# A memory-recurrent attention kernel: last projection rows two at a time, softmax sums in column tiles, a new order of work in a segment, weights loaded from the second quarter on

## The chip, the cores and the metric

The kernel runs on one core of one Trainium2 chip. The metric is the device time of a whole execution in microseconds; I give medians of several executions. The times of the kernel before lie within 0.3 to 0.8% of one another, by round (1616.15 to 1620.62 us in one of seven executions, 1615.40 to 1627.98 in another), those of a variant below, in its fast runs, within 0.1 to 0.9%. A profile shows one execution, and its span is some 2 us shorter than the time of the same execution (1627.2 us against 1628.95 for the changed kernel). The record counts all the timed runs that I compare as fast, except one that is named (1636.07 us at a granted clock of 0.957); the two kernels that had one look only have no state in it.

## The reference, cut to what matters

```python
# A: 64 segments of 32 tokens; an 8-token memory is carried from one segment to the next
for s in range(n_seg):
    h = concat([mem, x[:, 32 * s:32 * s + 32]])        # 40 tokens, 576 features
    q, k, v = h @ Wq, h @ Wk, h @ Wv                   # 32 heads of 128
    p = softmax(where(mask, q @ k.T * scale, -1e9))
    o = (p @ v) @ Wo
    mem, out = o[:8], o[8:]
# B: ordinary attention over 2048 tokens, 32 heads of 18
# result: g * A + (1 - g) * B with g = sigmoid(x . gate_w)
```

A is serial: a segment needs the memory of the one before. B is parallel, and the kernel cuts it into 512 steps (scores `sb`, exponential, values `ob`), of which it lays 7 or 8 beside each segment of A.

Of the kernel before, what the change touches and what calls it, by code (L numbers as in the profile page):

```python
# [16 lines left out]
def kernel(  # L17
# [77 lines left out]
    def weights(name):  # L95
        return (
            aw1.tile([P, NF, HD], BF16, name=name + "_m"),
            aw1.tile([P, HD // 2], BF16, name=name + "_t"),
        )

    wv, wq, wk = weights("wv"), weights("wq"), weights("wk")

    def load_weights(w, src):
        w2 = src.rearrange("d h e -> d (h e)")
        for c in range(NF):
            yield nc.gpsimd.dma_start(out=w[0][:, c, :], in_=w2[c * P:(c + 1) * P, :])
        for two in range(2):
            yield nc.gpsimd.dma_start(
                out=w[1][TL * two:TL * two + TL, :],
                in_=w2[NF * P:Dm, two * (HD // 2):(two + 1) * (HD // 2)],  # L110
            )

    def w_slice(w, c, f0, n):

        if c < NF:
            return w[0][:, c, f0:f0 + n], c
        f1 = f0 % (HD // 2)
        return w[1][:, f1:f1 + n], NF + f0 // (HD // 2)
# [143 lines left out]
    loads, first_loads = nc.sync, []  # L262
# [37 lines left out]
    def last_tokens(q, share, k=None):  # L300
# [8 lines left out]
        for b in range(HD // 512):  # L309
            pv = bank(k[0], [P, 512], FP32, "pv")  # L310
            for c in range(NF + 1):
                rw, cc = w_slice(wv, c, b * 512, 512)
                nc.tensor.matmul(pv[:, :], lhsT=xlb[:, cc, :], rhs=rw, start=(c == 0), stop=(c == NF))  # L313
            vl = stage()
            yield
            copy_out(vl[:, :], pv[:, :], share)
            store.dma_start(out=vld[q * P:(q + 1) * P, b * 512:(b + 1) * 512], in_=vl[:, :])
            yield
# [143 lines left out]
    for t in range(NQC):  # L462
        for n in range(4 * t, 4 * t + 4):
# [23 lines left out]

    load_first()
    ready.extend([first_loads[-1]] * 2)
# [23 lines left out]
    def between(cost):  # L513
        spare[0] += cost
        if spare[0] >= 1.8:
            spare[0] -= 1.8
            b_advance(1)

    for blk in FIRST:
        store_qk(blk, range(1, GB))  # L520
    for kb in range(NKB):
        project_vb(1, kb, 3)
# [10 lines left out]
    for q in range(4):  # L533
        in_turn(
            nc.gpsimd.dma_start(
                out=wo[:, 8 * q:8 * q + 8, :], in_=A_Wo[8 * q:8 * q + 8].rearrange("h e d -> e h d")
            )
        )
    fix = actx.enter_context(tc.tile_pool(name="fix", bufs=1))
    seg2 = actx.enter_context(tc.tile_pool(name="seg2", bufs=2))  # L540


    def pad(g):
        for t in (qtd, ktd):
            nc.gpsimd.dma_start(out=pads(t, g), in_=pads(t, 0))

    pad(1)


    for i, _ in enumerate(last_tokens(0, 1 << 30)):  # L550
        if i % 2:
            between(1.1)
    loads = nc.gpsimd

    fill_bank = [0]

    def later_tokens():
        for q in range(1, n_seg // SG):
            yield from last_tokens(q, 0, fill_bank)

    later = later_tokens()


# [70 lines left out]
    put_x(0)  # L634

# [102 lines left out]
    def segment(s, banks):  # L738
# [11 lines left out]
        def project(x, w, b, k):  # L750
            pv = bank(k, [P, 512], FP32, "pvv")
            for c in range(NF + 1):
                for j in range(4):
                    rw, cc = w_slice(w, c, (2 * (j // 2) + b) * 1024 + (j % 2) * 512, 512)
                    nc.tensor.matmul(  # L755
                        pv[32 * j:32 * j + 32, :],
                        lhsT=ht[:, cc, :],
                        rhs=rw,
                        start=(c == 0),
                        stop=(c == NF),  # L760
                        tile_position=(0, 32 * j),
                    )
            ps[x] = pv
# [56 lines left out]
        def sums(b, k):  # L820
            ps["p", b] = bank(k, [P, 512], FP32, "pss")
            nc.tensor.matmul(ps["p", b][:, 0:W8], lhsT=bsel[:, :], rhs=et[:, b, :], start=True, stop=True)  # L822
# [79 lines left out]
        for x, w in (("Q", wq), ("K", wk), ("V", wv)):  # L902
            for b in range(2):
                step(f"{x}{b}", project, f"{x}{b}", w, b, banks[f"{x}{b}"])
                step(f"c{x}{b}", copy, f"{x}{b}")
        for b in range(2):
# [30 lines left out]
        for i in range(3):  # L937
# [9 lines left out]
        Q0 cQ0 K0 B E : cK0 / K1 tq0 tk0 pq0 V0 cK1 B E : pk0 Q1 S0 cV0 v0 cQ1 x0 tk1 n0 B E : tq1 pk1  # L947
        V1 pq1 p0 cV1 v1 l0 r0 / S1 m0 B F1 w00 x1 n1 o00 F2 cF1 p1 w01 E : B l1 cF2 o01 r1 m1 E : F0
        a00 w10 cF0 w11 B E : o10 o11 ol a01 a10 a11 B / E : h0 g0 h1 g1 f0 ht0 f1 ht1 og oh
        """.split(),  # L950
        8: """
        Q0 B E : V0 cQ0 K0 cV0 v0 B / cK0 E : tq0 pq0 Q1 tk0 pk0 cQ1 B / E : S0 K1 tq1 x0 cK1 B n0 tk1 E
        : V1 pk1 pq1 p0 cV1 v1 S1 l0 r0 x1 / B E : F0 m0 n1 w00 o00 F1 cF0 p1 w01 o01 cF1 l1 r1 m1 B F2
        a00 cF2 w10 o10 w11 E : B E : o11 ol a01 a10 h0 a11 g0 B h1 g1 f0 E : f1 ht0 ht1 oh og
# [4 lines left out]
            A0=0, A1=1, F0=2, F1=0, F2=1, K0=2, K1=0, Q0=1, Q1=2, S0=0, S1=1, V0=1, V1=0, p0=2, p1=2,  # L959
            pv=0, pw=2, t0=2, t1=1, w00=2, w01=0, w10=1, w11=2,  # L960
        ),
        8: dict(
            A0=2, A1=0, F0=0, F1=1, F2=0, K0=0, K1=2, Q0=2, Q1=1, S0=0, S1=1, V0=1, V1=2, p0=0, p1=2,
            pv=0, pw=1, t0=2, t1=1, w00=2, w01=0, w10=1, w11=0,
# [3 lines left out]
    LOAD_LAST = "r1"  # L968
# [163 lines left out]
```

## The kernel before: the parts that the change touches

A segment projects its first 32 tokens here, in four column tiles; the last 8 tokens of every segment are projected ahead, for 16 segments together (`last_tokens`, the fill-in of the loop). Of the 576 rows of a weight, four chunks have 128; the last 64 take a fifth pass, in which half of the array works on zeros.

```python
def project(x, w, b, k):
    pv = bank(k, [P, 512], FP32, "pvv")
    for c in range(NF + 1):                 # NF = 4 full chunks and the last 64 rows
        for j in range(4):                  # four column tiles at a time
            rw, cc = w_slice(w, c, (2 * (j // 2) + b) * 1024 + (j % 2) * 512, 512)
            nc.tensor.matmul(pv[32 * j:32 * j + 32, :], lhsT=ht[:, cc, :], rhs=rw,
                start=(c == 0), stop=(c == NF), tile_position=(0, 32 * j))
    ps[x] = pv

def copy(x):
    sbt[x] = seg2.tile([P, 512], BF16, name="tm", bufs=4)
    nc.vector.tensor_copy(out=sbt[x][:, :], in_=ps[x][:, :])
```

The order of a segment is a list of names. `Q0` to `V1` are projections, `cQ0` their casts, `tq0`, `pq0` transposes of queries and their copies, `S` scores, `x`, `l`, `r` three ScalarE operations of the softmax, `n`, `m` two of VectorE, `p` sums, `w` weighing, `a` output projection, `f`, `ht` the next memory, `F1`, `F2` the fill-in, `B` and `E` the two halves of a step of B.

```python
8: """
Q0 B E : V0 cQ0 K0 cV0 v0 B / cK0 E : tq0 pq0 Q1 tk0 pk0 cQ1 B / E : S0 K1 tq1 x0 cK1 B n0 tk1 E
: V1 pk1 pq1 p0 cV1 v1 S1 l0 r0 x1 / B E : F0 m0 n1 w00 o00 F1 cF0 p1 w01 o01 cF1 l1 r1 m1 B F2
a00 cF2 w10 o10 w11 E : B E : o11 ol a01 a10 h0 a11 g0 B h1 g1 f0 E : f1 ht0 ht1 oh og
""".split(),
```

The start-up stores queries and keys, then the second half of the values, then projects the rest with steps of B between:

```python
for blk in FIRST:
    store_qk(blk, range(1, GB))
for kb in range(NKB):
    project_vb(1, kb, 3)
for blk in (1, 6, 2, 7, 3, 8):
    for t in range(NQC):
        project_qk(blk, t, 0)
        between(1.1)                        # a step of B when 1.8 us have gathered
# ... loads of Wo, padding copies, last tokens of 16 segments, then the set-up of the segments
```

The softmax here doesn't subtract the row's maximum and nothing guards it: scores larger than these inputs give would overflow.

## Time and profile before

| | kernel before |
|---|---|
| time, median | 1619.4 us |
| profiled span, mean granted clock | 1613.9 us, 0.986 |
| start of the first segment (first `Q0`) | 174.55 us |
| start of the last segment | 1558.28 us |
| segments with 7 steps | 28 of 64 |

The prediction below shows the main views. Two more are needed for the explanation, and I had not read them before I predicted. The first is busy time by stretch: window, length, then busy us of TensorE, weight loads, VectorE, ScalarE and GpSimd with their counts, then the granted clock (1.00 is full), DMA share and GB/s. The lines are 22 segments with 7 steps, 19 with 8 steps and fill-in, and the last 16 without fill-in.

```profile
174.55:657.68 483.13, 454.87 (x8119) 239.43 (x8119) 305.79 (x755) 339.67 (x286) 101.96 (x221) 0.99 0.22 52
789.15:1212.97 423.82, 409.63 (x7276) 213.78 (x7277) 265.48 (x663) 327.10 (x266) 87.20 (x190) 1.00 0.21 47
1212.97:1558.28 345.31, 315.00 (x5744) 160.33 (x5742) 210.18 (x537) 274.46 (x225) 55.50 (x130) 1.00 0.17 35
```

TensorE is busy for 409.63 of 423.82 us, 97%, in the second. The waits of TensorE in 680 to 1200 us agree (who waited, for whom: us in all, times, longest):

```profile
PE pw L879 <- DVE hl L657: 4.6, 15, 0.4
PE pvv L755 <- DVE ht L891: 4.4, 9, 0.5
PE sb L238 <- ACT etb L257: 4.2, 12, 0.6
```

All the waits of that view come to less than 20 us in 520.

### The profile page before, as it was taken

The numbers are of one execution on the slowest core, as the hardware profiler recorded it, in microseconds if no ns is written. First come the engines' busy times: TensorE is split into PE (matmuls) and PEld (weight loads), VectorE is DVE, ScalarE is ACT, GpSimd is POOL, SyncE is SP. The second block draws the span as 40 slices with busy tenths as digits, with TensorE's granted clock in tenths as the row PEclk, the third lists the DMA queues.
The fourth block names the chain that finished last, engine by engine and source line by source line (L and its number), as shares of the span: only waits on it lengthen the run. The fifth ranks groups of instructions, "written<-read, shape, count | busy, mean of one in ns | idle before, by whom it ended". The sixth has DMA issues, their size and how long they took to land.

```text
span 1613.9 us, 57766 instructions
## 1 busy us (share of the span) xinstructions
PE 1476.7 (91%) x25082; PEld 782.0 (48%) x25082; DVE 960.0 (59%) x2355; ACT 1139.8 (71%) x981; POOL 338.4 (21%) x731
## 2 busy tenths in 40 slices
PE   6598899999999999999999999999999989998997
PEld 3434444555454444555454445555554444444445
DVE  2233666666566666666566666666666656565656
ACT  2165577777677767777677777777777777788774
POOL 6311211213131031302121211212121212120131
PEclk9899999999999999999999999999999999999999
DMA  7788322212122121212122121212221121211125
GB/s 200 235 291 290 100 65 64 49 42 52 45 50 53 32 53 38 61 36 49 43 43 60 38 50 40 57 39 45 51 53 35 30 48 34 45 34 35 29 59 162
DMA packets 209865, 114.39 MB, mean 71 GB/s; under 512 B 159491, under 2 KB 197251, under 8 KB 208019
## 3 DMA queue, kind: packets, MB, share of 16 engines
q1 hardware_dynamic: 188971, 58.40, 16.1%
q0 software_dynamic: 19696, 50.02, 9.9%
q8 instruction: 196, 3.21, 0.9%
q10 hardware_dynamic: 944, 2.29, 0.4%
q14 instruction: 58, 0.48, 0.1%
HBM read 60.94 MB, written 36.10 MB: 60 GB/s over the span
## 4 chain that ended last, share of the span: by engine, by line
PE 69%; ACT 11%; DVE 11%; DMA 4%; issue 2%; SPq 1%; POOL 1%; DVEq 0%; ACTq 0%; POOLq 0%
PE pvv L755 27%; ACT etb L257 9%; PE sb L238 8%; PE ob L222 7%; PE pt L782 5%; PE pv L326 4%; PE psh L800 3%; PE acc L643 3%; PE pso L838 3%; PE pv L313 2%; DVE hl L657 2%; PE pq L420 2%; DVE hl L654 2%; DVE ot L850 2%; ACT rq L830 2%
## 5 line engine op out<-in xcount | busy, mean ns | idle before, releaser
L257 ACT ACTIVATE etb<-sb 128x2048 bf16<-128x2048 f32 x512 | 959.6, 1874 | 341.9 <-PE sb L238 341.1
L767 DVE CAST tm<-pvv 128x512 bf16<-128x512 f32 x384 | 264.4, 689 | 175.1 <-PE pvv L755 174.2
L755 PEld LDWEIGHTS <-ht 128*32 128x32 bf16 x7680 | 185.8, 97 | 183.7 <-DVE ht L891 14.1
L238 PE MATMUL sb<-qch,kch 32*128 32x512 bf16 x2048 | 203.2, 386 | 38.5 <-ACT etb L257 36.7
L222 PE MATMUL ob<-etb,vch 128*32 128x512 bf16 x2048 | 205.9, 392 | 3.9 <-DVE tq L159 3.9
L850 DVE CAST ot<-pso 128x320 bf16<-128x320 f32 x256 | 120.7, 488 | 104.2 <-PE pso L838 99.9
L643 PE MATMUL acc<-wo,ot 128*32 128x384 bf16 (+1 forms) x4096 | 159.7, 291 | 5.4 <-DVE ot L850 3.3
L755 PE MATMUL pvv<-wq_m,ht 128*32 128x512 bf16 x2048 | 134.2, 382 | 13.0 <-DVE ht L891 8.3
L755 PE MATMUL pvv<-wk_m,ht 128*32 128x512 bf16 x2048 | 134.9, 384 | 0.0
L755 PE MATMUL pvv<-wv_m,ht 128*32 128x512 bf16 x2048 | 134.3, 382 | 0.0
L643 PEld LDWEIGHTS <-ot 128*32 128x32 bf16 x4096 | 105.2, 98 | 46.5 <-DVE ot L850 12.8
L700 POOL DMA_DIRECT2D a_dram<-rl x186 | 92.6, 506 | 162.4 <-DVE rl L695 143.3
L238 PEld LDWEIGHTS <-kch 32*128 32x128 bf16 x2048 | 61.2, 91 | 128.5 <-issue 107.9
L857 POOL COPY otl<-ot 128x256 bf16<-128x256 bf16 x64 | 25.9, 405 | 445.6 <-DVE ot L850 445.6
L222 PEld LDWEIGHTS <-vch 128*32 128x32 bf16 x2048 | 52.9, 93 | 120.6 <-issue 116.0
L782 PE MATMUL pt<-ident,tm 128*128 128x128 bf16 x1024 | 96.8, 221 | 0.8 <-DVE tm L767 0.8
L790 DVE COPY kt<-pt 128x512 bf16<-128x512 bf16 x128 | 54.0, 422 | 69.4 <-PE pt L782 69.0
L838 PE MATMUL pso<-et,v_sb 64*128 64x40 bf16 x2048 | 81.4, 178 | 14.9 <-DVE hll L657 4.7
L838 PEld LDWEIGHTS <-v_sb 64*128 64x128 bf16 x2048 | 62.8, 93 | 62.4 <-issue 49.5
L654 DVE CAST hl<-acc 128x384 bf16<-128x384 f32 (+1 forms) x128 | 57.9, 452 | 58.1 <-PE acc L643 57.8
L782 PEld LDWEIGHTS <-tm 128*128 128x128 bf16 x1024 | 57.8, 98 | 67.0 <-issue 49.4
L826 ACT ACTIVATE lt<-pss 128x320 f32<-128x320 f32 x128 | 56.0, 438 | 43.2 <-PE pss L822 32.8
(141 smaller groups left out, 1847.4 us busy)
## 6 DMA issues: line engine op xcount, KB each, us to landing
v_sb<-tm SPq DMA_DIRECT2D x512, 32.0 KB
wo<-in_A_Wo_dram POOLq DMA_DIRECT2D x4, 1152.0 KB, 9.7
wv_m<-in_A_Wv_dram POOLq DMA_DIRECT2D x4, 1024.0 KB, 8.0
wq_m<-in_A_Wq_dram POOLq DMA_DIRECT2D x4, 1024.0 KB, 9.1
wk_m<-in_A_Wk_dram POOLq DMA_DIRECT2D x4, 1024.0 KB, 8.0
xl<-qld SPq DMA_DIRECT2D x64, 64.0 KB
xl<-kld SPq DMA_DIRECT2D x64, 64.0 KB
v_sb<-vld SPq DMA_DIRECT2D x128, 32.0 KB
```

Of the source, the lines that this page charges most:

```text
L222: nc.tensor.matmul(ob[32 * j:32 * j + 32, :], lhsT=vc[:, o + 32 * j:o + 32 * j + 32], rhs=et4[:, j, :], start=(kb == 0), stop=(kb == NKB - 1),
L238: nc.tensor.matmul(sb[:, j, :], lhsT=kc[32 * j:32 * j + 32, o:o + P], rhs=qch[gq][32 * j:32 * j + 32, :], start=True, stop=True, tile_posi ...
L257: nc.scalar.activation(out=before[:, :, :], in_=sb[:, :, :], func=ACT.Exp, scale=scale_b)
L326: nc.tensor.matmul(pv[:, o:o + P], lhsT=lw, rhs=xlb[:, cc, :], start=(c == 0), stop=(c == NF))
L643: nc.tensor.matmul(acc[32 * j:32 * j + 32, 0:d1 - d0], lhsT=o[:, h, 0:CT], rhs=wo[:, h, d0:d1], start=(b == 0 and i == 0), stop=(b == 1 an ...
L654: nc.vector.tensor_copy(out=hl[:, 0, d0:d1], in_=acc[:, 0:d1 - d0])
L700: eng.dma_start(out=rows4[m, seg - LO:seg, i * n:(i + 1) * n], in_=rl[32 * i + m * LO:32 * i + (m + 1) * LO, :],)
L755: nc.tensor.matmul(pv[32 * j:32 * j + 32, :], lhsT=ht[:, cc, :], rhs=rw, start=(c == 0), stop=(c == NF), tile_position=(0, 32 * j),)
L767: nc.vector.tensor_copy(out=sbt[x][:, :], in_=ps[x][:, :])
L782: nc.tensor.transpose(out=pt[:, which, :, :, :].rearrange("p j (u i) t -> p j u i t", i=4)[:, :, :, i, :], in_=sbt[x][:, i * Dh:(i + 1) * Dh],
L838: nc.tensor.matmul(pso[:, i * L:(i + 1) * L], lhsT=v_sb[64 * jj:64 * jj + 64, b * 1024 + i * Dh:b * 1024 + (i + 1) * Dh], rhs=et[64 * jj:6 ...
L850: nc.vector.tensor_copy(out=ot[:, j * HG:(j + 1) * HG, :].rearrange("p h t -> p (h t)"), in_=ps["o", b, jj][:, 0:W8],)
```

## The change

Its intent: two projections share one pass for their last 64 rows, one in the upper and one in the lower half of the array, so that six tail passes become three; softmax sums and the fill-in's values are cut into column tiles like their neighbours, so that the tile shape changes less often; a new order puts the first projections and steps densely one after another; in the start-up, part of the weights is loaded between 20 and 60 us, the values are stored ahead of queries and keys, fewer steps of B stand there, and the set-up of the segments goes ahead of the last tokens. The core of the diff:

```diff
-        def project(x, w, b, k):
-            pv = bank(k, [P, 512], FP32, "pvv")
-            for c in range(NF + 1):
+        def project(x, w, b):
+            first = begin(x)
+            for c in range(NF):
                 ...
+        def project_tails(two):
+            two = [(x, w, b, begin(x)) for x, w, b in two]
+            for j in range(4):
+                for x, w, b, first in two:
+                    t, r = w_tail(w, columns(b, j), 512)
+                    nc.tensor.matmul(
+                        ps[x][32 * j:32 * j + 32, :],
+                        lhsT=ht[TL * r:TL * r + TL, NF + r, :],
+                        rhs=t[TL * r:TL * r + TL, :],
+                        start=first, stop=(not first),
+                        tile_position=(TL * r, 32 * j),
+                        skip_group_check=True,
+                    )
... (sums and the fill-in's values: one matmul becomes four column tiles)
+        step("T0", project_tails, (("Q0", wq, 0), ("K0", wk, 0)))
+        step("T1", project_tails, (("Q1", wq, 1), ("K1", wk, 1)))
+        step("T2", project_tails, (("V0", wv, 0), ("V1", wv, 1)))
... (order of 8 steps; that of 7 likewise)
-        Q0 B E : V0 cQ0 K0 cV0 v0 B / cK0 E : tq0 pq0 Q1 tk0 pk0 cQ1 B / E : S0 K1 tq1 x0 cK1 B n0 tk1 E
-        : V1 pk1 pq1 p0 cV1 v1 S1 l0 r0 x1 / B E : F0 m0 n1 w00 o00 F1 cF0 p1 w01 o01 cF1 l1 r1 m1 B F2
-        a00 cF2 w10 o10 w11 E : B E : o11 ol a01 a10 h0 a11 g0 B h1 g1 f0 E : f1 ht0 ht1 oh og
+        Q0 B T0 / cQ0 V1 T2 E : cV1 v1 B E : V0 K0 cV0 v0 B E : Q1 cK0 tk0 / tq0 T1 pq0 B K1 E : cQ1 pk0
+        cK1 S0 tq1 x0 B E : pq1 tk1 n0 pk1 S1 x1 p0 / l0 r0 n1 F1 p1 m0 cF1 F0 cF0 l1 r1 m1 B E : w00
+        w01 o00 o01 w11 w10 a00 B E : o10 o11 a01 h0 g0 a10 a11 F2 ol h1 B g1 cF2 E : f0 ht0 f1 ht1 oh
+        og
... (start-up)
+        for _ in range((0, 1, 2, 2)[t]):
+            next(pieces)                    # pieces of the weights, from the second quarter on
-        if spare[0] >= 1.8:
-            spare[0] -= 1.8
+        if spare[0] >= 2.15:
+            spare[0] -= 2.2
+    for kb in range(NKB):
+        project_vb(1, kb, 3)
     for blk in FIRST:
         store_qk(blk, range(1, GB))
-    for kb in range(NKB):
-        project_vb(1, kb, 3)
... (loads of Wo, padding copies and the last tokens move behind the set-up of the segments)
```

## The prediction

> **What bounds the kernel now.** I read the page, then busy time by stretch, then the timeline and the chain of waits of each stretch. The run has three stages: a start-up up to 174.5 us (transposes, projections of attention B, last tokens of the first 16 segments), 64 recurrent segments up to about 1572 us, and the final projection. The chain that ended last is mainly TensorE:
>
> ```profile
> PE 69%; ACT 11%; DVE 11%; DMA 4%; issue 2%; SPq 1%; POOL 1%; DVEq 0%; ACTq 0%; POOLq 0%
> ```
>
> Each segment carries 7 or 8 steps of attention B: scores `sb`, one 1.88 us exponential on ScalarE, values `ob`. The segments from 174.55 us on take 21.95 us on average with 7 steps (28 segments), the other 36 about 22.0. A packed stretch of one with 8 (timeline, TensorE: start, length, line):
>
> ```profile
> 901.71 1.05 PE L755 MATMUL pvv<-wq_m,ht 128*32 128x512 bf16 x16
> 902.58 0.39 PE L755 MATMUL pvv<-wq_t,ht 128*32 128x512 bf16 x4
> 902.90 0.40 PE L238 MATMUL sb<-qch,kch 32*128 32x512 bf16 x4
> 903.23 0.40 PE L222 MATMUL ob<-etb,vch 128*32 128x512 bf16 x4
> 903.45 1.04 PE L755 MATMUL pvv<-wv_m,ht 128*32 128x512 bf16 x16
> 904.32 0.39 PE L755 MATMUL pvv<-wv_t,ht 128*32 128x512 bf16 x4
> 904.53 1.04 PE L755 MATMUL pvv<-wk_m,ht 128*32 128x512 bf16 x16
> ```
>
> Ends are modelled, so read start to start. Sixteen projection matmuls, four passes of four concurrent column tiles, take 0.87 us, 0.217 a pass. A pass followed by the same tile shape takes 0.21 (904.32 to 904.53), one followed by another shape 0.32 or 0.33 (902.58 to 902.90). So a change of tile shape costs 0.107 us. Adding passes and shape changes by these figures gives 20.0 us for a 7-step segment and 20.9 for an 8-step one. The rest is waiting. Busy time by stretch of two 8-step segments, one with fill-in projections and one of the last 17, when these have run out:
>
> ```profile
> 901.71:924.14 22.43, 21.53 (x359) 10.30 (x358) 13.95 (x35) 18.05 (x15) 7.91 (x16) 1.00 0.18 38
> 1537.24:1558.28 21.04, 18.86 (x341) 9.51 (x342) 12.66 (x34) 16.73 (x15) 1.44 (x5) 1.00 0.13 24
> ```
>
> TensorE (second figure) does 2.7 us less in the second, which is only 1.4 us shorter: **TensorE is not the only bound of a segment**. ScalarE's period is one: score buffer free, 0.50 us from the start of `sb` to the exponential, 1.88, 0.05 back, together 2.43 us, as between 97.62 and 100.06 us in ScalarE's timeline. Eight of these are 19.4 us, and the recurrence (softmax, weighing, output, next memory) runs beside them.
>
> The start-up is bound elsewhere (chain of waits, 40 to 90 us; waits; busy time by stretch):
>
> ```profile
> 68.19 8.86 DMA ktd<-stg
> 77.11 8.90 DMA vgd<-vt
> ```
> ```profile
> PE pvb L447 <- DVE xn L291: 16.0, 1, 16.0
> DVE xn L291 <- DMA vgd<-xn: 16.9, 2, 16.7
> ```
> ```profile
> 60.00:86.00 26.00, 10.04 (x58) 6.00 (x56) 2.60 (x6) 1.20 (x3) 2.71 (x5) 0.67 0.91 299
> ```
>
> TensorE stood 16 us because the value buffers were full: their stores lay in the SP queue behind the query and key stores, while weights loaded and the DMA engines were 91% busy.
>
> [...] Here four row tiles (`sb`) and four column tiles each take one pass (0.217 us without the change); eight at once no run shows yet. [...] earlier weights move traffic, they don't remove it.
>
> **The change, part by part.**
>
> 1. Tails. The last 64 of 576 rows cost each of six projections a full pass with half the array on zeros: 6 x 0.217 = 1.30 us a segment. Now two projections share one pass, in the upper and lower row half: 3 x 0.217 = 0.65. Saved 0.65 us of TensorE a segment.
>
> 2. Shape changes. Softmax sums and value last tokens become 128x32 and sit beside other 128x32 work; the tails are a new shape, three times. Counting along the instruction order: 29 to 31 changes in a 7-step segment become 27 to 29, 32 to 34 in an 8-step one 30 to 33. One or two of 0.107 saved, 0.15 us. Parts 1 and 2: 20.0 to about 19.1 us (7), 20.9 to about 20.0 (8). Over 63 segments, with point 4, the count falls from 1260 to 1211 us.
>
> 3. New order. I walked one segment of each kind along the queues, with the trace's durations and hand-overs (0.12 us TensorE to VectorE, 0.05 back, 0.50 `sb` to exponential). **7 steps:** TensorE stays packed to the seventh step; waits remain at the third to fifth step, before the second weighing and at the end: 20.4 us, 20.7 with division work in VectorE's queue, against 21.95. That mean holds seven segments of 22.7 to 24.5, in several of which VectorE's transpose `tq`, waiting for `ob` at the head of its queue, holds up the memory path for 1.3 us or so; in the new order it lies better. **8 steps:** the first five steps now come every 2.43 us, ScalarE's period. The second scores must wait for a key copy behind the fifth step (starting about 12.3 us in, against 11.6 before), then five small ScalarE operations and the weighing follow in series. I get 21.9 to 22.2 us with fill-in, against 22.2, and about 21.5 without, against 21.6. Here nearly all of the 0.9 us turns into waits.
>
> 4. Steps of B in the start-up fall from 29 to 24 (threshold 1.8 to 2.15, always two projections to a step), so 41 segments have eight instead of 36. Cost 5 x about 1.5 = 7 us in the loop, within these sums: before 1558.28 - 174.55 = 1384 us to the last segment; after 23 x 20.7 + 24 x 22.1 + 16 x 21.5 = 1350. **Loop: -33 us.**
>
> 5. Start-up. Value stores go ahead, so the 16 us wait shrinks to 1 to 3. Queries and keys then wait for a staging buffer (15 stores x 0.36 us issue after the values, plus 5 us landing): second-half projections run from about 73 us instead of 83 to 87. Then 12 pairs at 2 x 1.09 + 0.65 + changes = 2.92 us make 35 (before: 24 projections and 16 steps in 40 us, with single projections leaving ScalarE's 2.43 us exposed). A new wait: the segment set-up, moved ahead of the last tokens, puts the memory transposes behind the load `m0`, itself behind the last key stores on SP: about 7 us. Last tokens: 12 pairs at 2.9 = 35, plus 2 to 3 us for slow stores, against 46.4 before, and the 3.4 us set-up wait at 171 goes. Segment 0 starts at about 73 + 36 + 7 + 38 = 154 instead of 174.5. **-20 us.** Five weight pieces (4.25 MB, about 15 us at 290 GB/s) now fall between 20 and 60 us, where DMA is 63 to 68% busy. They fit, for about 2 us lost.
>
> 6. End. The final loads start after K1, earlier, so the last segment's value stores no longer meet them (its weighing waited 3 us on `v_sb<-tm`). **-3 us.**
>
> Sum -33 - 20 - 3 = -56; 1619 - 56 = 1563 us.
>
> **Rivals.**
> - *All of the TensorE count arrives*: waits a segment stay as they were (1384 - 1260 = 124 us), loop 1211 + 124 = 1335, total about 1547. For it: the 7-step segments were packed. Against: the 1.4 of 2.7 us above.
> - *ScalarE and the recurrence become the bound*: 8-step segments 0.5 us slower than before, 7-step ones only 0.5 us faster; loop about 1390, only start-up and end pay: about 1600. For it: the 2.43 us period and five more 8-step segments.
> - *The start-up wait only moves* to the staging buffers, `m0` and slow stores under the earlier weights: 8 us instead of 20, about 1575.
> - *Eight tiles do not run at once*: a tail costs two passes, 3 x 0.217 x 64 = 42 us more on TensorE, partly in existing waits; about 1595.
>
> **Range and chances.** Loop -33 +- 18, start-up -20 +- 9, end -3 +- 2 give 1540 to 1588. Faster by over 2% needs less than 1587, which start-up plus a third of the loop gain reaches: 0.88. Within 2%: 0.11, the second or fourth rival. Slower needs both and no start-up gain: 0.01.
>
> **What would show it.** Tail groups of eight with 0.32 us start to start; segment 0 at 150 to 158 us; no 16 us wait on the value buffers, but waits before the memory transposes of about 7; 7-step segments near 20.7 and 8-step ones near 22; exponentials 2.43 us apart in the first half of an 8-step segment, with "TensorE waits for ScalarE" grown. Wrong if 8-step segments come to 21.3 or less (time near 1540), or if tails take 0.5 us.

## The result and the profile after

The changed kernel took 1632.05 us (median of 4, 1628.95 to 1633.78) against 1619.39 us of the kernel before on the same chip (4 runs). Ratios here are the mean time of one kernel's fast runs over that of the other's of the same rounds, so not quite the ratio of the medians: 1.0076, interval 1.0050 to 1.0101. It is slightly slower, where I had predicted 1563.

The chain that ended last, and the granted clock in 40 slices of the span (9 is 90% or more):

```profile
PEclk9997999999999999999999999999999998898999
...
PE 54%; DVE 14%; ACT 10%; DMA 9%; issue 6%; SPq 3%; POOL 2%; DVEq 0%; ACTq 0%; POOLq 0%
```

Before, TensorE had 69% of this chain and DMA 4%; now a DMA share of 9% and slices below 9 near the end of the loop stand out. Busy time by stretch, after (start-up, then the same three kinds of segments):

```profile
0.00:174.97 174.97, 129.41 (x1184) 72.58 (x1191) 60.55 (x118) 61.99 (x77) 60.78 (x117) 0.89 0.74 243
174.97:642.21 467.24, 441.38 (x8491) 233.03 (x8490) 298.16 (x750) 339.69 (x287) 95.94 (x209) 1.00 0.24 54
781.08:1206.27 425.19, 396.08 (x7511) 209.42 (x7511) 266.43 (x668) 328.20 (x267) 90.18 (x196) 1.00 0.21 48
1206.27:1570.83 364.56, 331.71 (x5838) 162.38 (x5838) 209.31 (x536) 276.71 (x225) 56.09 (x131) 0.92 0.17 33
```

The 7-step stretch is 16 us shorter. In the 8-step stretch TensorE is busy 13.55 us less than before and the stretch is 1.4 us *longer*. In the last sixteen TensorE is busy 17 us *more*, with less work, at a clock of 0.92: matmuls that take longer at half clock count as busy all the while (one output projection took 2.72 us there, and 1.49 in a run whose clock held; both timelines stand below).

The waits of TensorE in the start-up, and those of the 8-step stretch (660 to 1180 us):

```profile
PE ptm L612 <- DMA m<-in_A_mem_dram: 10.9, 1, 10.9
PE ob L233 <- DVE tq L170: 10.2, 1, 10.2
PE pq L439 <- DVE stg L302: 7.5, 1, 7.5
...
```
```profile
PE psh L849 <- DVE kt L839: 15.7, 29, 0.8
PE pvv L789 <- DVE ht L948: 6.3, 11, 0.6
```

The 16 us wait on the value buffers is gone. Three waits have 28.6 us in its place; those for `m` and for `stg` ahead of `pq` are new, that of `ob` for `tq` was 3.9 us before. In the loop a wait for the key copies `kt` has appeared that the kernel before did not have. The shared tails themselves work (TensorE's timeline: start, length):

```profile
1005.84 0.39 PE L804 MATMUL pvv<-wq_t,ht 64*32 64x512 bf16 x1
...
1006.18 1.05 PE L789 MATMUL pvv<-wv_m,ht 128*32 128x512 bf16 x16
...
1007.16 0.41 PE L804 MATMUL pvv<-wv_t,ht 64*32 64x512 bf16 x8
```

Eight matmuls in 0.34 us start to start (1005.84 to 1006.18), the change of shape of 0.107 included: they do run at once.

Where the predicted sum missed, from the starts of the segments in the profiled run:

| term | predicted | measured | miss |
|---|---|---|---|
| start of segment 0 | 154 | 175.0 | +21 |
| 23 segments with 7 steps | 23 x 20.7 = 476 | 493.0 | +17 |
| 24 with 8 steps and fill-in | 24 x 22.1 = 530 | 538.3 | +8 |
| 16 with 8 steps, without | 16 x 21.5 = 344 | 364.6 | +21 |
| from the start of the last segment | 55.6 - 3 = 52.6 | 56.4 | +4 |

The sum is 71 us; the times differ by 1632 - 1563 = 69.

To see what the loop's segments are made of, I divide each stretch into the waits of TensorE that the profile records and the rest (work, changes of shape, issue gaps), in us per segment:

| | 7 steps (22) | 8 steps with fill-in (19) | last 16 |
|---|---|---|---|
| before: length = wait + rest | 21.96 = 1.13 + 20.83 | 22.31 = 0.74 + 21.57 | 21.58 = 1.84 + 19.74 |
| after | 21.24 = 1.02 + 20.22 | 22.38 = 1.34 + 21.04 | 22.78 = 1.91 + 20.88 |

(The stretch of 22 leaves out the last 7-step segment, where the order changes: it took 25.7 us after. In the kernel before the last 7-step segment took 24.5 and the one behind it 23.6. A wait of up to 0.15 us is not recorded as one and counts as rest. In every fourth segment the output projection of the last tokens stands in place of the fill-in.)

### The profile page after: what moved, and what is told of

Its sections match the earlier page's. It is cut to its first block, busy times and chain, and to the rows that moved or that the text cites. A ratio compares the mean times of both kernels' runs of the same rounds, so it can differ in the third digit from the quotient of the medians.

```text
span 1627.2 us, 59554 instructions
## 1 busy us (share of the span) xinstructions
PE 1469.0 (90%) x25939; PEld 772.4 (47%) x25946; DVE 951.4 (58%) x2355; ACT 1140.5 (70%) x981; POOL 344.9 (21%) x740
## 4 chain that ended last, share of the span: by engine, by line
PE 54%; DVE 14%; ACT 10%; DMA 9%; issue 6%; SPq 3%; POOL 2%; DVEq 0%; ACTq 0%; POOLq 0%
PE pvv L789 14%; PE sb L249 8%; PE acc L668 7%; ACT etb L268 7%; PE ob L233 5%; PE pv L345 4%; DMA v_sb<-tm 3%; PE psh L849 3%; PE pt L831 3%; DVE ot L907 3%; SPq L821 2%; PE pvv L804 2%; POOL a_dram L725 2%; DVE hl L682 2%; DVE hl L679 2%
## 5 line engine op out<-in xcount | busy, mean ns | idle before, releaser
L789 PEld LDWEIGHTS <-ht 128*32 128x32 bf16 x6144 | 154.4, 96 | 150.7 <-DVE ht L948 17.9
L249 PE MATMUL sb<-qch,kch 32*128 32x512 bf16 x2048 | 206.9, 391 | 7.9 <-ACT etb L268 4.5
L668 PE MATMUL acc<-wo,ot 128*32 128x384 bf16 (+1 forms) x4096 | 168.0, 311 | 3.5
L789 PE MATMUL pvv<-wk_m,ht 128*32 128x512 bf16 x2048 | 128.7, 379 | 0.0
L249 PEld LDWEIGHTS <-kch 32*128 32x128 bf16 x2048 | 65.3, 91 | 132.5 <-issue 110.9
L914 POOL COPY otl<-ot 128x256 bf16<-128x256 bf16 x64 | 25.7, 402 | 470.1 <-DVE ot L907 261.3
L907 DVE CAST ot<-pso 128x320 bf16<-128x320 f32 x256 | 115.3, 485 | 9.2 <-PE pso L895 5.9
L849 PE MATMUL psh<-qt,kt 128*64 128x40 bf16 x2048 | 74.5, 189 | 34.3 <-DVE kt L839 30.3
L849 PEld LDWEIGHTS <-kt 128*64 128x64 bf16 x2048 | 61.5, 112 | 76.1 <-DVE kt L839 56.0
L839 DVE COPY qt<-pt 128x512 bf16<-128x512 bf16 x128 | 53.7, 419 | 60.0 <-PE pt L831 56.7
L831 PE MATMUL pt<-ident,tm 128*128 128x128 bf16 x1024 | 87.0, 222 | 0.0
```

Source lines behind the costliest of these rows:

```text
L249: nc.tensor.matmul(sb[:, j, :], lhsT=kc[32 * j:32 * j + 32, o:o + P], rhs=qch[gq][32 * j:32 * j + 32, :], start=True, stop=True, tile_posi ...
L668: nc.tensor.matmul(acc[32 * j:32 * j + 32, 0:d1 - d0], lhsT=o[:, h, 0:CT], rhs=wo[:, h, d0:d1], start=(b == 0 and i == 0), stop=(b == 1 an ...
L789: nc.tensor.matmul(ps[x][32 * j:32 * j + 32, :], lhsT=ht[:, c, :], rhs=w[0][:, c, columns(b, j):columns(b, j) + 512], start=(first and c = ...
L831: nc.tensor.transpose(out=pt[:, which, :, :, :].rearrange("p j (u i) t -> p j u i t", i=4)[:, :, :, i, :], in_=sbt[x][:, i * Dh:(i + 1) * Dh],
L849: nc.tensor.matmul(psh[64 * jj:64 * jj + 64, i * L:(i + 1) * L], lhsT=kt[:, h * L:h * L + 64], rhs=qt[:, h, :], start=True, stop=True, til ...
L907: nc.vector.tensor_copy(out=ot[:, j * HG:(j + 1) * HG, :].rearrange("p h t -> p (h t)"), in_=ps["o", b, jj][:, 0:W8],)
```

## The experiments

All are the changed kernel with one edit unless it says otherwise. "Half clock" is the time in which the trace's clock records show half of full speed. The record marks all results as agreeing with the reference, the two that are wrong on purpose included, so its check does not notice half an exponential.

### The loop: tails, the exponential, the key copies

**Tails undone.** Each projection does its own fifth pass again; the new order stays.

```diff
-            for c in range(NF):
+            for c in range(NF + 1):
+                    rw, cc = w_slice(w, c, columns(b, j), 512)
         def project_tails(two):
+            return
```

> The changed kernel with part 1 alone undone: each of the six projections does its own fifth pass again, in the same new order. Theory (the 8-step segments are bound by ScalarE's 2.43 us period and the recurrence, and TensorE has waits to spare): the 3 x 0.217 = 0.65 us a segment of TensorE come back mostly into waits; 7-step segments 0.3 to 0.6 us longer (23 of them), 8-step ones with fill-in 0.2 to 0.4, and those of the last 16 no longer or even shorter[...]: the time 5 to 20 us above the changed kernel's. Rival (TensorE bounds every segment, the tails were worth their full count): 64 x 0.65 = 42 us longer, about 1674 us.

Measured: 1648.42 us, ratio to before 1.0192 (1.0170 to 1.0214), so by the ratios 19 us slower than the changed kernel. The segments: 21.14 = 0.67 + 20.47 (7 steps), 22.91 = 1.81 + 21.11 (8 with fill-in), 23.50 (last 16). In TensorE's own time the shared tails save only 20.47 - 20.22 = 0.25 us with 7 steps and 0.07 with 8, not 0.65. The timeline of this run shows a full tail pass and its change of shape:

```profile
1015.87 1.04 PE L790 MATMUL pvv<-wq_m,ht 128*32 128x512 bf16 x16
1016.73 0.39 PE L790 MATMUL pvv<-wq_t,ht 128*32 128x512 bf16 x4
1017.05 0.62 PE L833 MATMUL pt<-ident,tm 128*128 128x128 bf16 x8
```

A tail within its projection costs 0.217 us, and the change behind it (0.32 - 0.217) is due anyway. A shared one costs 0.34 to 0.36, because it brings a change of its own. Three against six: 3 x 0.35 = 1.05 against 1.30, 0.25 saved. (With 8 steps the tail of the values is followed by the next matmul only after 0.46 us, as in the lines above from 1007.16; that leaves 0.14, and why 0.07 was measured stays open.) That they are worth 19 us all the same is a matter of waits (8-step segments 0.47 us more of them without) and of the last sixteen.

**Half of the exponential**, wrong on purpose: ScalarE computes two of four quarters, the rest of the buffer holds ones. Once on the changed kernel, once on the kernel before.

```diff
-                nc.scalar.activation(out=before[:, :, :], in_=sb[:, :, :], func=ACT.Exp, scale=scale_b)
+                nc.scalar.activation(out=before[:, 0:2, :], in_=sb[:, 0:2, :], func=ACT.Exp, scale=scale_b)
```

> Wrong on purpose: the changed kernel with B's exponential over half of the scores (two of four banks; the other half of its buffer constant), so that one takes about 1 us instead of 1.88 and ScalarE's period falls from 2.43 to about 1.55 us. Theory (8-step segments are bound by ScalarE's period): those with fill-in fall from 22.4 to 20.4 to 21.2 us, close to TensorE's count of 20.1 to 20.3, and 7-step ones from 21.4 to 20 to 20.8. Rival (the waits are those of the recurrence alone): 8-step segments with fill-in stay above 21.8.

> Wrong on purpose: the same half exponential in the kernel before. TensorE's count is 20.9 us for an 8-step segment there. Theory: with ScalarE out of the way the count bounds, 8-step segments with fill-in go from 22.3 to 21.3 to 21.8 us, and the changed kernel's lead in them, nothing in the real kernels, becomes 0.5 to 0.9 us. Rival (recurrence alone): both kernels stay where they were, lead under 0.3 us.

Measured, one look each: 1616.11 and 1605.66 us. The 8-step segments with fill-in went from 22.38 to 22.10 (after) and from 22.31 to 22.30 (before), though the operation took 1.02 instead of 1.88 us. The theory that ScalarE's 2.43 us period bounds these segments falls. Most of what the two whole times fell came from other segments: on the kernel before those with 7 steps (21.96 to 21.62) and the last sixteen (21.58 to 21.27), on the changed one the last sixteen (22.78 to 22.15, with 41.0 us of half clock).

**The order around the key copies.** The first key copy ahead of the cast of the second queries, the second key transposes ahead of the fifth step.

```diff
-   ... tq0 T1 pq0 B K1 E : cQ1 pk0
-        cK1 S0 tq1 x0 B E : pq1 tk1 n0 pk1 S1 x1 p0 ...
+   ... tq0 T1 pq0 B K1 E : pk0 cQ1
+        cK1 S0 tq1 tk1 x0 B E : pq1 pk1 n0 S1 x1 p0 ...
```

> The changed kernel with two moves in its order for eight steps: the first key copy (VectorE) stands ahead of the cast of the second queries, not behind it, and the second key transposes (TensorE) stand ahead of the fifth step instead of behind it. Nothing else differs. Theory (the TensorE time that the change saved in an 8-step segment is spent waiting for these key copies; in the trace of the changed kernel TensorE waits 0.8 us a segment for them, and 1.34 us in all against 0.74 before): the 8-step segments with fill-in go from 22.38 to about 21.8 us, their waits from 1.34 to about 0.8, the sixteen without from 22.78 to about 22.2, or lower if their waits were also what halved the clock; total 1610 to 1620 against 1632 of the changed kernel. Rival (the recurrence as a whole is as long as the segment, a shorter wait here comes back later as a wait for the softmax or for the next memory): 22.3 and 22.7, total about 1630.

Measured: 1636.68 us, 1.0124 (1.0092 to 1.0156). The wait went, the time did not (660 to 1200 us):

```profile
PE pvv L789 <- DVE ht L948: 6.9, 12, 0.6
PE pso L895 <- DVE et L890: 4.6, 12, 0.6
PE psh L849 <- DVE kt L839: 4.4, 23, 0.2
PE pso L895 <- DVE oseg L740: 3.6, 6, 0.6
PE pss L872 <- DVE et L864: 3.2, 17, 0.3
```

8-step segments 22.54 = 1.14 + 21.40, last sixteen 23.08. The rival held: 11 us of waiting for keys were taken away, waits for the softmax and for a copy (`oseg`) took the place of some 7 us of them, and the half clock grew, by 10 us in these segments and by 10 in the last sixteen. My theory that this wait *is* the lost gain was wrong; it was one form of it.

**Five buffers for the casts.** In the new order both values are cast early, and the cast of the second queries takes over the buffer of a value tile, whose four stores must land first (6.4 us in eight casts between 660 and 1180 us, VectorE's waits).

```diff
-   seg2.tile([P, 512], BF16, name="tm", bufs=4)        # both places
+   seg2.tile([P, 512], BF16, name="tm", bufs=5)
-   qch[i] = bint.tile([P, QC], BF16, name="qch", bufs=3)
+   qch[i] = bint.tile([P, QC], BF16, name="qch", bufs=2)
```

> The changed kernel with five instead of four buffers for the casts of the projections (and two instead of three for the queries of B, which makes the room). In the changed order of eight steps the cast of the second queries takes over the buffer of the second values and so waits for their four stores: 6.4 us in eight of the 23 segments between 660 and 1180 us. Theory that this wait is a main part of the lost gain: these casts no longer wait for the stores, the 8-step segments with fill-in fall from 22.38 to about 22.1, total about 1622. Rival (the wait is there but the key copy behind it is late anyway, for the casts and transposes ahead of it): at most 0.1 us a segment, 22.3, total about 1629.

Measured: 1616.23 us, 0.9992 (0.9968 to 1.0016), by the ratios 14 us better than the changed kernel, more than the rival said and some more than the theory. 8-step segments 22.21, between the two. The largest single part (6.6 of 14.3 us between the two profiled spans) came from a place that I had not thought of: the last tokens of the start-up use the same buffers, and there the 10.2 us wait shrank:

```profile
PE ptm L612 <- DMA m<-in_A_mem_dram: 12.1, 1, 12.1
...
PE ob L233 <- DVE tq L170: 4.2, 1, 4.2
```

Segment 0 started at 168.4 instead of 175.0.

### The start-up

**Set-up of the segments back** behind the last tokens; and **the same with the padding copies behind segment 0** (`pad` copies DRAM to DRAM, four at a time at 137 to 140 us, while the stores of the last tokens run).

```diff
# e_setup: the block from "for q in range(4): in_turn(... wo ...)" to "later = later_tokens()" where it was before
# e_startfix: as e_setup, and
-    pad(1)
...
+        if s == 0:
+            pad(1)
```

> The changed kernel with the segment set-up put back behind the last tokens, and the output weights' loads ahead of it, as before. Theory (the memory transposes' 10.9 us wait for their load, behind the key stores on SP, is a wait that this move made, and half clock follows it): last tokens start about 114 us instead of 125, the old wait of 3 us at the end comes back: segment 0 at 165 to 169 instead of 175, time 6 to 10 us lower. Rival (the wait is only moved on, to the stores of the last tokens that share the engines with the weights): segment 0 at 173 to 176, time within 3 us.

> The changed kernel with the set-up put back behind the last tokens (as in e_setup) and all padding copies within DRAM (qtd<-qtd, ktd<-ktd, 10 to 12 us each to landing) issued only once segment 0 has started. Theory (these copies make the store vld<-tm land after 14 us, which held TensorE 10 us through the queue of VectorE): last tokens go on without that wait, segment 0 at 155 to 160 us instead of 165 in e_setup and 175 in the changed kernel: time 12 to 18 us below the changed kernel, about 1612 to 1618. Rival (the store is slow because the output weights load beside it): segment 0 at 163 to 168, as e_setup, about 1620.

Measured: 1620.37 us, 1.0016 (0.9986 to 1.0047), and 1617.77 us, 0.9956 (0.9902 to 1.0009; one of its four runs was slow, 1636.07 at a clock of 0.957, and is left out of the ratio). Segment 0 started at 165.2 and 159.5 instead of 175.0. Moving the set-up, and with it the wait for the load of `m0`, is thus worth some 10 us. The step from 165.2 to 159.5 must not be put down to the padding copies: three runs with the very same start-up (this one and two below) had 159.5, 167.9 and 164.3, so single starts are good to 4 us or so, and the two ratios overlap. The traces speak against the theory as well. The store of the last tokens that the chain of work runs through took 9.3 us in the run with the padding copies (it landed before they were issued), and 8.6 and 9.8 us in two runs in which no such copy ran ahead of segment 0. Stores are slow here without them; that they make one slower is not shown.

**No early weights.**

```diff
-        for _ in range((0, 1, 2, 2)[t]):
-            next(pieces)
```

> The changed kernel without the five early weight pieces: all weights load after the first loads of B. Theory (they are moved traffic: they delayed the input rows, 9.6 us from issue to landing near 38 to 47 us, and the stores behind, by 2 to 5 us, and gave nothing back, since no engine waits for a weight): second-half projections start 2 to 5 us earlier, but the weights now meet the stores of queries and keys, 90 to 120 us: segment 0 within 4 us of the changed kernel's, time within 5 us. Rival (the early weights are what makes the start-up bearable): segment 0 8 us later or more.

Measured: 1630.61 us, 1.0071 (1.0040 to 1.0101), as the changed kernel itself; segment 0 at 174.0. Loading five pieces earlier moved traffic and bought nothing.

### The last sixteen segments: the clock

**Useless matmuls** where the fill-in has run out, five of 512 columns at each of its two places, 28 us in all; on the changed kernel and on the kernel before.

```diff
-        next(later, None)
+        if next(later, "end") == "end":
+            pd = bank(k, [P, 512], FP32, "dum")
+            for c in range(5):
+                nc.tensor.matmul(pd[:, :], lhsT=ident[:, :], rhs=wo[:, c, 0:512], start=(c == 0), stop=(c == 4))
```

> The changed kernel with useless work: where the fill-in projections have run out (13 of the last 17 segments), two groups of five 128x512 matmuls on a spare PSUM bank, 2 x 1.08 us a segment, result unused. Theory (in these segments TensorE's waits let its clock fall to half for 3.4 or 6.8 us at a time; 11 such windows of 61 us in all after 1180 us in the changed kernel's trace): the windows go, segments come to 22.0 to 22.5 us as those with fill-in, the 16 segments from 48 on take 355 us instead of 365: the time 7 to 12 us lower, with more work. Rival (these segments are slow for the order of their waits, the clock has no part): 0.5 to 1 us longer each, time 5 to 20 us higher.

> Control: the same useless work in the kernel before, whose clock stays full there (one window of 3.4 us after 1180 us). Both theories: its last 16 segments go from 21.58 to about 22.1 us each, time 5 to 10 us higher than before.

Measured: 1627.46 us, 1.0063 (1.0023 to 1.0103), and 1625.28 us, 1.0044 (1.0030 to 1.0059). On the kernel before, 28 us of work cost 10 us (last sixteen from 21.58 to 22.20). On the changed kernel they made the last sixteen *shorter*, 22.78 to 22.48, and the half clock in them went from 61.4 us to nothing. (The whole run gained some 2 us by the ratios, where 7 to 12 were expected; its segment 0 started 3 us later.) So half clock is the loss there: 61.4 us at half speed is by my estimate at most 31 us of lost work, nearly 2 us a segment; the runs below get some 20 us of it back.

**Combinations.** With the start-up repaired and the new key order, without and with these matmuls:

> Three parts together: the set-up of the segments back behind the last tokens and the copies of the padding behind the first segment (as in the run that repaired the start-up), and the two moves in the order of eight steps. Theory (start-up and loop losses are independent and add): start of the first segment near 160 us, 8-step segments with fill-in near 21.8, total about 1617.8 - 35 x 0.5 = 1600, a gain of over 1% against the kernel before. Rival (the clock takes it back: sparser segments run at half clock for longer, above all the last sixteen): half clock after segment 47 of 80 us and more, total 1612 to 1620.

> The same with 28 us of useless matmuls in the segments that have no fill-in left. Theory of the clock (half clock costs the last sixteen segments nearly 2 us each and sparse work is what brings it): no half clock after segment 47, these segments at 22.2 us or less, and total 3 to 8 us below the same kernel without them, about 1595. Rival (with the shorter waits of the new order the clock holds up by itself): the useless matmuls then only cost, about 10 us as they did in the kernel before, total 1610.

Measured: 1625.39 us, 1.0046 (1.0020 to 1.0072), with 75 us of half clock after segment 47, and 1610.8 us, 0.9960 (0.9931 to 0.9989), with none. The key order was a burden here too, so I dropped it and took the five buffers in its place:

> The changed kernel with the set-up of the segments back behind the last tokens, the padding copies behind the first segment, and five buffers for the casts of the projections (the three repairs that helped alone, the order untouched). Theory (start-up losses are the load of the memory, the padding copies and the buffers of the casts; in the loop the buffers): start of the first segment 153 to 160 us, 8-step segments with fill-in 22.2, the last sixteen near 22.8 with 60 to 75 us of half clock; total about 1605. Rival (the repairs overlap, all three wait for the same transfers): start 160 to 165, total about 1615.

Measured: 1609.34 us, 0.9936 (0.9895 to 0.9977); the profiled run is the slowest of its five, 1616.17. Segment 0 at 162.3, 8-step segments 22.21, half clock after segment 47 still 71.7 us, last sixteen 22.77. Then one place filled, the other, both:

```diff
# e_topF1: only between the second scores and the sums;  e_topF2: only behind the output projection
+        if next(later, "end") == "end" and i == 1:      # i == 2 in e_topF2
```

> The same with useless matmuls at the first place of the fill-in only (five of 512 columns, between the second scores and the first softmax sums, 14 us over the last sixteen segments). Theory that the place matters (the clock falls where the waits for the second key copy and for the softmax lie close together, and this is that place): half clock after segment 47 below 10 us, segments near 22.0, total 6 to 10 us below the same kernel without. Rival (only the sum of the work in a segment matters): half the filling takes away half of the half clock, about 35 us left, and the total moves by 2 us or less.

> The same with the useless matmuls at the second place only (between the last scores of B and the next memory's folding, behind the output projection), again 14 us. Theory that the place matters: half clock after segment 47 stays at 50 us or more, and the run is as slow as the one without or slower. Rival (the sum of the work): the same as with the first place only, about 35 us of half clock.

> The same with both places filled, 28 us. From the run that did this to the changed kernel: no half clock after segment 47, the last sixteen at 22.4 us. Theory: total 4 to 8 us below the kernel without fillings, about 1599, and 1% below the kernel before. If one place is enough, this one is 5 us slower than that. Rival (the fillings do not pay where the waits for buffers are gone): equal to the kernel without.

And the first place with two matmuls instead of five:

> The best kernel so far (three repairs, five useless matmuls at the first place) with two useless matmuls there instead of five: 0.44 us instead of 1.08 a segment, which is shorter than the wait for the softmax that it fills (up to 0.7 us). Theory (the clock falls for the wait that stands at this place, so filling that wait is enough): half clock after segment 47 below 14 us, the last sixteen segments 21.3 to 21.7, total 1584 to 1590. Rival (the clock needs the full 1.08 us there): half clock 30 us or more, segments near 22.3, total near 1600.

| last sixteen segments | time, us | ratio to before | half clock, us | us a segment |
|---|---|---|---|---|
| none filled | 1609.34 | 0.9936 | 71.7 | 22.77 |
| second place, 5 | 1616.10 | 0.9988 | 64.9 | 23.44 |
| both, 5 and 5 | 1601.46 | 0.9898 (0.9864 to 0.9932) | 0 | 22.28 |
| first place, 5 | 1590.42 | 0.9825 (0.9790 to 0.9861) | 0 | 21.70 |
| first place, 2 | 1589.05 | 0.9811 (0.9794 to 0.9829) | 3.4 | 21.51 |

The same amount of work in the first place brings 1.1 us a segment, in the second it costs 0.7. The place decides, not the sum. Why, the timeline shows; first the changed kernel:

```profile
1218.75 0.58 PE L849 MATMUL psh<-qt,kt 128*64 128x40 bf16 x16 [0.52 <-DVE kt L839]
1219.26 0.32 PE L872 MATMUL pss<-et,bsel 128*32 128x320 bf16 x4
1220.30 0.32 PE L872 MATMUL pss<-et,bsel 128*32 128x320 bf16 x4 [0.71 <-DVE et L864]
...
1225.25 2.72 PE L668 MATMUL acc<-wo,ot 128*32 128x384 bf16 x48
```

and the best kernel at the same point of its segment:

```profile
1205.47 0.60 PE L761 MATMUL dum<-wo,ident 128*128 128x512 bf16 x2
1206.25 0.32 PE L875 MATMUL pss<-et,bsel 128*32 128x320 bf16 x4 [0.18 <-DVE et L867]
...
1210.17 1.49 PE L666 MATMUL acc<-wo,ot 128*32 128x384 bf16 x48
```

The output projection takes 2.72 us in the one and 1.49 in the other. In the clock records of the changed kernel the half clock comes in pieces of 3.41 us or a multiple (3.41 to 13.65 us, but for a last one that the end of the trace cuts), and its starts in the loop lie whole multiples of 3.41 us apart. So I cut the loop into windows of that length, on the grid of these starts (busy time by stretch; second figure TensorE, the clock third from the end):

```profile
1214.16:1217.57 3.41, 3.41 (x66) 1.74 (x63) 2.50 (x6) 2.74 (x3) 0.00 (x0) 1.00 0.19 48
1217.57:1220.98 3.41, 2.18 (x41) 1.15 (x40) 1.28 (x5) 3.23 (x5) 0.00 (x0) 1.00 0.43 43
1220.98:1227.81 6.83, 6.73 (x108) 3.64 (x104) 3.09 (x8) 4.32 (x4) 1.86 (x5) 0.50 0.10 30
```

The window with both waits was busy for 2.18 of 3.41 us, 64%, and the next two ran at half clock. A window of the best kernel at the same place, 1.2 us ahead of the second scores in both, was busy for 2.71 us, 79%, and the clock held:

```profile
1203.50:1206.91 3.41, 2.71 (x45) 1.27 (x42) 1.28 (x5) 3.21 (x5) 0.00 (x0) 1.00 0.40 41
```

On the changed kernel's grid every one of the eleven windows ahead of a half-clock piece in the last sixteen segments was busy for 0.64 to 0.75; windows of 0.78 and more were never followed by one there. Not every sparse window was followed by one: four were not, of 0.64 (from 1538.4 us), 0.68 (from 1238.0), 0.75 and 0.77. In the kernel before, the last sixteen segments have twenty windows of 0.63 to 0.77 that were *not* followed by one, and one of 0.71 that was. So the busy time of the profile alone does not tell them apart.

Another count fits better. If each matmul's columns are weighted by the part of the array that the matmul uses (a tile of 64 rows and 32 columns is an eighth of it), a window's work can be estimated in full passes of 512 columns, of which 15.7 fit in at the 0.217 us that one takes in these traces. The window from 1217.57 us has 4.9 such passes, the best kernel's 6.9, two of them useless. In the last sixteen segments the windows ahead of half clock have 3.9 to 6.1 on the changed kernel and 4.8 on the one before; the twenty of the kernel before that were let pass have 5.4 to 10.0, that of 0.68 has 7.6; the one of 0.64 at 1538.4 us stays an exception with 4.4. From the first segment's start to the last one's, in these two traces together, half clock followed 14 of 18 windows with less than 5.5 passes and 3 of 772 others; a cut by busy time at 0.70 gives 13 of 21 and 4 of 769. This count is an estimate of mine, made from the traces afterwards, and no run tested it: it fits these two traces, and what brings the half clock is not shown.

Where the sparse window comes from can be read off the orders. In the old order `K1` and `V1` stand amid the softmax of the first heads, large matmuls between small ones. In the new order all six projections are done before the second scores; the softmax then has only the fill-in beside it, and where that has run out, nothing. The changed kernel's own trace holds a check of this. Segments 48, 52, 56 and 60 have the output projection of last tokens there, 32 real matmuls at the first place (segment 52):

```profile
1333.88 0.58 PE L849 MATMUL psh<-qt,kt 128*64 128x40 bf16 x16 [0.52 <-DVE kt L839]
1334.39 0.32 PE L872 MATMUL pss<-et,bsel 128*32 128x320 bf16 x4
1334.54 1.47 PE L668 MATMUL accl<-wo,otl 128*32 128x384 bf16 x32
```

No half-clock piece starts in any of these four; of the other twelve of the last sixteen, eleven have one.

**The steps moved out of the start-up**, on the kernel with five matmuls at the first place:

```diff
-        if spare[0] >= 2.15:
-            spare[0] -= 2.2
+        if spare[0] >= 1.8:
+            spare[0] -= 1.8
```

> The best kernel so far (five useless matmuls) with the threshold of the kernel before for steps of B in the start-up, so that 29 instead of 24 lie there and 36 segments instead of 41 have eight steps. The prediction put the five moved steps at 1.5 us each in the loop, 7 us, against two projections to a step in the start-up. Theory that they are worth their price in the loop (7-step segments measured at 21.3, 8-step ones at 22.2): loop 4 to 5 us shorter, start-up 3 to 5 us longer, total within 3 us of 1590. Rival (in the start-up single projections leave ScalarE's period exposed): start-up 8 to 10 us longer, total 1594 to 1597.

Measured: 1592.45 us, 0.9825 (0.9800 to 0.9850), level with 1590.42. Segment 0 started at 168.5 (five runs with the threshold of the change and this start-up: 155.0 to 162.9), and the five segments that went back to 7 steps took 106.7 instead of 111.8 us. Moving five steps is an even exchange; the threshold is no cause of the miss.

## Why the prediction was wrong

1. **"20.0 us for a 7-step segment and 20.9 for an 8-step one. The rest is waiting."** This is the step that failed in the loop. My count of passes and changes was 0.8 and 0.7 us too low for the kernel before: 20.83 and 21.57 measured, with waits of 1.13 and 0.74 us only. I took the difference for waiting that a better order could use. The view of an 8-step segment that I quoted myself had TensorE busy for 21.53 of 22.43 us. The argument from 2.7 against 1.4 us compared it with a segment *without* fill-in, which does wait (1.84 us), and carried the conclusion over. (The 1260 us for 63 segments do not follow from 20.0 and 20.9 either: 28 x 20.0 + 35 x 20.9 is 1292; the count of the last sixteen that makes up the difference is not shown.)

2. **Saved TensorE time, 0.9 us a segment.** It was 0.61 (7 steps) and 0.53 (8). The term that was mis-sized is the tail: 0.65 predicted, 0.25 and 0.07 measured, since each shared tail brings its own change of shape. I had counted the changes over the whole order, where those of the tails and those that the order saves were added up. The rest of the saving (0.36 and 0.46) came from the order and the column tiles, more than the 0.25 that parts 1 and 2 left for it; this is a remainder, not a run of its own.

3. **7-step segments.** The mechanism held: nearly all that TensorE saved arrived, waits stayed at 1.0 us. Of the 0.54 us between 20.7 and the measured 21.24, 0.29 is the oversized saving; the rest is waiting that the new order was to remove and that went from 1.13 to 1.02 only. In the sum over 23 segments (+17) the one long segment of 25.7 us has 5.

4. **8-step segments with fill-in.** That the gain would turn into waits was right, in size too (22.38 against 21.9 to 22.2). The reason was not: halving the exponential moved 0.3 us of it at most, in the kernel before nothing. TensorE's saving of 0.53 was met by 0.60 of new waits, most of them for the key copies, on VectorE, in part behind casts that wait for value stores. So "TensorE is not the only bound" came true once its work was less. The wait that shows is not the cause by itself: with it taken away others came. Five buffers brought 0.17 us back.

5. **The last sixteen: 21.5 predicted, 22.78 measured.** No step of mine had the clock in it. With the clock kept up by two useless matmuls (and the five buffers, which alone leave these segments at 22.65) they take 21.51: the clock is the miss of 21 us. That the walk gave the same 21.5 shows its sum, not each of its waits. The new order made one window of the segment sparse; elsewhere the fill-in stood there (clock 1.00 over the 19 segments that have it).

6. **Start-up: 154 predicted, 175 measured.** The 16 us wait went as predicted, but I had sized the waits that followed it too small. By stretches: the second-half projections began at 80.9 instead of 73 (7.5 us of waiting for a staging buffer), took 32.6 us instead of 36, `m0` cost 10.9 instead of 7, and the last tokens took 50.6 instead of 38: 7.9 - 3.4 + 3.9 + 12.6 = 21 us. In the last of these, slow stores cost 10.2 us instead of 2 to 3 (one store took 14.2 us from issue to landing), and two half-clock pieces (10.24 us from 118.5, 13.65 us from 145.8) stretched the two groups of matmuls in them by some 2 us each (4.14 and 4.38 us, where the groups behind them took 2.16 and 2.34). I had no term for the clock. The rival "the start-up wait only moves" was right, and larger than I had it. In the repaired runs, with the wait for `m0` gone and most of the others shorter, segment 0 starts at 155 to 163.

7. **End: -3.** Nothing came of it; 56.4 against 55.6 us.

8. **Tails of eight at once**: right, 0.34 us against 0.32. Early weights as moved traffic: right, 1630.61 us without them against 1632.05.

What stays open: what brings the half clock, for which the weighted passes are only a fit; what is behind the one long segment where the order changes from 7 to 8; and whether real work put at the first place (a piece of B, or `V1` back amid the softmax) would also gain time; with real work there, in segments 48, 52, 56 and 60, no piece of half clock started. The best kernel here, 1589.05 us, is 1.9% faster than the kernel before and 2.6% faster than the changed one.

## What to carry to other kernels

Before counting on saved engine time, read the engine's recorded waits in the stretch: here they were 0.74 of 22.31 us, 3%, TensorE was the bound, and the count that said otherwise had left out 0.7 us. But the next bound can be close behind: here 0.53 us saved on an engine that was 97% busy came back as 0.60 us of new waits. When projections are packed together, look at what is left in the thinnest few microseconds of the loop: here two waits of 0.52 and 0.71 us with small matmuls between them, in one window of 3.41 us, stood ahead of 6.83 us of half clock, and the 61.4 us of it in the last sixteen segments cost by my estimate nearly 2 us a segment, where the packing saved 0.5 to 0.6. A little work put exactly there, useless work even, paid for itself: with two matmuls, 0.44 us a segment, the ratio went from 0.9936 to 0.9811. The wait of 16 us that was removed from a queue of transfers gave way to three others in the start-up, 28.6 us together, so follow the buffers to the end before booking the gain.
